# Streaming attention and a max-out MLP on one core: flags through a one-row matmul, batch 0's evacuations shared out anew, and another order for the weight preparation

## The chip, the cores and the metric

The kernel runs on one core of a Trainium2 chip. The time is the device time of one execution in microseconds (us), as the median of several runs. The profile is of a single further execution, and its times are counted from the first instruction. The engines are TensorE (PE, with its weight loads PEld), VectorE (DVE), ScalarE (ACT), GpSimd (POOL) and SyncE (SP, which here only issues transfers).

## The reference

There are 4 batches, 8 heads, 768 positions and 64 numbers per head. For every batch and head:

```
scores = q k^T / 8
mask   = causal                                          (retrieval heads)
       = causal and (key < 4 or query - key < 64)        (all other heads)
a      = softmax(scores where mask, else -1e9)
x      = a v
```

The heads of a position are joined to a row of 512 numbers, which makes 3072 rows. Then come the weights w1 and w2 (512 x 1024) and w_out (1024 x 512):

```
out = max(x w1, x w2) w_out
```

Which heads are retrieval heads is an input (`is_retrieval`, 8 numbers of 64 bits). All inputs and the output are 32-bit floats in HBM.

## The kernel before, in words

**Algebra.** max(h1, h2) is written as relu(x (w1 - w2)) + x w2. So the MLP needs only one up-projection, with `w12 = w1 - w2`, and the term x w2 w_out is folded into the down-projection by the product `w2o = w2 w_out`. Both are made on the chip from the loaded weights: `cast_w` makes bf16 copies `w2b` and `wob`, `diff_w` makes the four row blocks of `w12`, `prep_w2t` transposes `w2b` on TensorE (8 steps of 4 transposes, tile `pw`, then `w2t`), and `prep_w2o` multiplies (4 steps of 8 matmuls of 512 columns, tile `pw2`, shown as `pw` in the profile).

**Attention.** The work goes by pairs of heads: 16 pairs, numbered 0 to 15, four to a batch. q, k and v of a pair are loaded by SP (`qn`, `kn`, `vn`, four buffers each), cast to bf16 (`cast_qk`, `cast_v`), and q and k are turned so that the 64 numbers of a head lie on partitions. For pairs 0 to 7 `turn` does this with six transposes on TensorE and an evacuation from PSUM by `evac` (tile `qkt`; first q with dst 0, then k with dst 1); for pairs 8 to 15 `turn_qk` does it with a transposing DMA on SP's queue. Only the 21 of 36 blocks of 128 x 128 on or under the diagonal are computed, in six chunks (`CHUNKS`) of four blocks, one of them of a single block. Chunk t is chunk t mod 6 of pair t // 6. Its steps are `scores` (TensorE, PSUM tile `ps`, two buffers), `expo` (ScalarE, tile `at`, six buffers), `mask` (VectorE, for the first four chunks of a pair) and `weighted` (TensorE, PSUM tile `po`, with a column of ones for the sum of each row); after the second and the sixth chunk `normalise` (VectorE) writes `x`.

**Masks.** `masks(h)` makes one head's table `msk` as `tab_a * r[h] + tab_b`, with `tab` a constant table that is loaded once and `r` the head's flag, the same on all 128 partitions. For blocks far from the diagonal v itself is scaled: `vf = vb * rj` (GpSimd).

**MLP.** `turn` (batch 0 and the last pair) or `turn_x` (a transposing DMA on SP) makes `xt`, the rows x with their 512 numbers on partitions. A batch has two groups of 384 rows. `up` (8 steps to a group, 4 matmuls of 384 columns each, tile `ph`) is evacuated with a relu into `g`; `down` (3 blocks of 128 rows to a group, 12 matmuls of 512 columns each, in four parts of three, tile `pout`) adds x w2o and g wob, is evacuated into `ot` and stored by SP.

**Order.** Everything is issued in program order, by hand; each engine and SP's queue take their instructions strictly in that order. Chunks are pipelined two ahead. Batch 0 runs alone (t from 0 to 23). From batch 1 on a small planner (`fill`, `step`) puts parts of the MLP of the batch before between the chunks: `shorts` are single steps and `longs` are the down-projections; a down-projection is not begun while a short of the same number waits. `turns` are turns that wait for one of two PSUM banks. `evac` gives each evacuation to VectorE or ScalarE, whichever has been given less estimated time so far.

Between batch 0 and batch 1 the kernel before does, in this order: two `prep_w2t` steps within each of t = 20 to 23; the loads of pairs 4 to 7; the four differences; one product step; the turn of batch 0's last x; the other three product steps; the 8 ups of the first group; casts and turns of pair 4. The 8 ups of the second group and all downs are left to the planner.

Of the kernel before, what the change touches and what calls it, by code (L numbers as in the profile page):

```python
# [34 lines left out]
def kernel(  # L35
# [56 lines left out]
    ident = tab[:, 0:128]  # L92
    tab_a = tab[:, 130:642]
    tab_b = tab[:, 642:1154]
    ir = consts.tile([128, 2 * H], I32)
    flag = consts.tile([128, 2 * H], F32)
    r = consts.tile([128, H], F32)
    rj = consts.tile([128, H, 4], BF16)
    sink = consts.tile([128, 1], F32)
# [33 lines left out]
        given["s"] += us  # L133
        return nc.scalar

    def evac(out, in_, cols, relu=False):
        if given["v"] <= given["s"]:
            eng = vec(0.16 + cols / 960)
            if relu:
                eng.tensor_scalar_max(out=out, in0=in_, scalar1=0.0)  # L140
            else:
                eng.tensor_copy(out=out, in_=in_)  # L142
        else:
            sca(0.2 + cols / 1300).activation(  # L144
                out=out, in_=in_, func=ACT.Relu if relu else ACT.Copy
            )
# [39 lines left out]
    def turn(n, dst, bank):  # L186
        s = st[n]
        src = s["qk"][:, dst] if dst is not None else s["x"]
        pt = bank("pt").bitcast(BF16)
        for i in range(NB):  # L190
            nc.tensor.transpose(  # L191
                pt[:, i * 128:(i + 1) * 128],
                src[:, i].rearrange("p h d -> p (h d)"), ident,
            )
        if dst is None:
            b, p = pairs[n]
            if p == 0:
                xts[b] = xtp.tile([128, KC, S], BF16, tag="xt", name="xt")
            t = xts[b][:, p, :]
        else:  # L200
            if dst == 0:
                s["qkt"] = qktp.tile([128, 2, S], BF16, tag="qkt", name="qkt")
            t = s["qkt"][:, dst]
        pt = pt[:, 0:S]
        if dst is not None:
            pt = pt.rearrange("p (n t) -> p t n", n=NB)
            t = t.rearrange("p (t n) -> p t n", n=NB)
            evac(t, pt, S)
        else:
            evac(t, pt, 400)  # L210

    def cast_qk(n, e, eng):
        s = st[n]
# [162 lines left out]
    def bank_d(name):  # L376
        return psum_m.tile([128, 512], F32, tag="m1", name=name)
# [124 lines left out]
    def masks(h):  # L502
# [6 lines left out]


    ir_handle = bass.AP(
        tensor=_as_int32(is_retrieval, 2 * H), offset=0, ap=[[0, 128], [1, 2 * H]]
    )
    nc.scalar.dma_start(out=ir, in_=ir_handle)
    load_one(0, "qn", q, nc.sync)
    nc.scalar.dma_start(out=tab, in_=table_dram.ap())
    load_one(0, "kn", k, nc.sync)
    load_one(0, "vn", v, nc.sync)
    for n in range(1, HP):
        load_pair(n)  # L520
    load_w(moe_w2, w2f, 0, 2)
    load_w(moe_w2, w2f, 2, 4)
    load_w(moe_w_out, wof, 0, 4)
    load_w(moe_w_out, wof, 4, 8)
    for kc in range(KC):
        load_w(moe_w1, w1f, kc, kc + 1)

    nc.vector.tensor_single_scalar(out=flag, in_=ir, scalar=0.0, op=ALU.not_equal)
    halves = flag.rearrange("p (h two) -> p h two", two=2)
    nc.vector.tensor_tensor(out=r, in0=halves[:, :, 0], in1=halves[:, :, 1], op=ALU.max)  # L530
    nc.vector.tensor_copy(out=sink, in_=tab[:, 128:129])
    nc.vector.tensor_scalar(
        out=rj[:, :, 0], in0=r, scalar1=sink, scalar2=None, op0=ALU.max
    )
    nc.vector.tensor_copy(
        out=rj[:, :, 1:4], in_=r.unsqueeze(2).to_broadcast([128, H, 3])
    )
    masks(0)
    cast_qk(0, 0, nc.vector)
    turn(0, 0, bank_a)  # L540
    cast_qk(0, 1, nc.vector)
    turn(0, 1, bank_d)
    masks(1)
    masks(2)
    cast_v(0, nc.gpsimd)
    masks(3)
    cast_qk(1, 0, nc.vector)
    cast_qk(1, 1, nc.gpsimd)

    T = NCH * len(pairs)  # L550
    T0 = NCH * HP

    def side(t, last, first_batch):
# [8 lines left out]
                turns.append((0.34, lambda bank: turn(m, 1, bank), 0))  # L562
        if m + 1 < last:
            if m + 1 < LONG and c == 5:
                cast_qk(m + 1, 0, nc.vector)
                cast_qk(m + 1, 1, nc.gpsimd)
            if m + 1 >= LONG and c == 2:
                cast_qk(m + 1, 0, nc.gpsimd)
                cast_qk(m + 1, 1, nc.gpsimd)
# [21 lines left out]
    for t in range(T0):  # L591
# [13 lines left out]
        if t == 15:  # L605
            for kc in range(KC):
                cast_w(nc.gpsimd, w2b, w2f, kc, kc + 1)
            for f2 in range(4):
                cast_w(nc.gpsimd, wob, wof, 2 * f2, 2 * f2 + 2)
        if 20 <= t:  # L610
            for fc in range(2 * (t - 20), 2 * (t - 20) + 2):
                prep_w2t(fc, (bank_a, bank_d)[fc % 2])
    weighted(T0 - 1)
    for n in range(HP, HP + 4):
        load_pair(n)
    diff_w(nc.gpsimd, 0)
    diff_w(nc.gpsimd, 1)
    diff_w(nc.vector, 2)
    diff_w(nc.vector, 3)
    prep_w2o(0, bank_d)  # L620
    turn(HP - 1, None, bank_a)
    for kc in range(1, KC):
        prep_w2o(kc, six[kc + 1])
    given["v"] = given["s"] = 0.0
    for e, u in enumerate(ups(0, 0)):
        u[1](six[e % 6])
    n = HP
    cast_qk(n, 0, nc.vector)
    cast_qk(n, 1, nc.vector)
    turn(n, 0, bank_a)  # L630
    turn(n, 1, bank_d)
    cast_v(n, nc.vector)
    cast_qk(n + 1, 0, nc.vector)
    cast_qk(n + 1, 1, nc.gpsimd)

# [5 lines left out]
                + sum(u[0] for u in turns))  # L641

    longs += downs(0, 0) + downs(0, 1)
    shorts += ups(0, 1)
    fill(1.3)
    scores(T0)
    scores(T0 + 1)
    expo(T0)
    fill(0.65)
    expo(T0 + 1)  # L650
    mask(T0)
    mask(T0 + 1)
# [84 lines left out]
```

## Time and profile before

| | |
|---|---|
| median of 3 runs | 221.22 us (221.1 to 221.78) |
| profiled execution, its own time | 222.22 us |
| its span, first to last instruction | 220.4 us |
| mean granted TensorE clock | 0.969 |
| TensorE busy | 187.3 us (85%) |
| VectorE busy | 121.6 us (55%) |
| ScalarE busy | 114.2 us (52%) |
| GpSimd busy | 66.0 us (30%) |

An engine is busy while one of its own instructions runs; issuing transfers and waiting are not counted. The profile names an instruction by its line and its tiles, as out<-in. A row of a timeline holds the start, the duration, the engine (with q for the queue that only issues), the line, the operation, the tiles, the shapes, the count, and in brackets how long the engine had been idle and what released it. A row of the busy time by stretch holds the stretch and its length, then for PE, PEld, DVE, ACT and POOL the busy time and the number of instructions, and at the end the granted clock of TensorE, the busy share of the DMA engines and GB/s.

### The profile page before, as it was taken

Reading aid. Unit: us, or ns where it says so; the run is one execution under the profiler, and the core shown is the slowest. Engines: PE = TensorE matmul, PEld = TensorE weight load, DVE = VectorE, ACT = ScalarE, POOL = GpSimd, SP = SyncE. Lnnn points to the kernel's source line nnn. Section 1 sums busy time; section 2 is a strip of 40 time slices with the busy share of each in tenths; the row PEclk is TensorE's granted clock in tenths of the full one; section 3 lists DMA queues with packets and bytes.
Section 4 is the critical chain, followed back from the end, with each engine's and each line's share of the span. In section 5 each row is a group of like instructions: output and inputs, shape, how many; then the busy total and the mean of one; then the engine's idle time right before and its main releaser. Section 6 shows DMA issues by size and latency. Waiting matters only on the chain.

```text
span 220.4 us, 4437 instructions
## 1 busy us (share of the span) xinstructions
PE 187.3 (85%) x1822; PEld 105.9 (48%) x1822; DVE 121.6 (55%) x222; ACT 114.2 (52%) x150; POOL 66.0 (30%) x72
## 2 busy tenths in 40 slices
PE   0268968499958889994999999999999999899993
PEld 0234745274534546552545555555545555455441
DVE  0699857964347769657286565666373631342101
ACT  2087898423347786885534566593644651232120
POOL 1194549940046082516064143315110000000000
PEclk9999999859999999999599999999999999999999
DMA  3999999995000939999999999979531331200222
GB/s 102 313 293 319 396 398 384 288 292 136 0 0 3 220 77 210 141 215 190 223 220 207 224 203 232 261 145 206 146 83 50 83 85 48 95 0 3 95 95 95
DMA packets 81300, 37.36 MB, mean 169 GB/s; under 512 B 71936, under 2 KB 76032, under 8 KB 81280
## 3 DMA queue, kind: packets, MB, share of 16 engines
q1 hardware_dynamic: 80992, 36.77, 72.4%
q8 instruction: 14, 0.23, 0.5%
q10 hardware_dynamic: 288, 0.30, 0.4%
q14 instruction: 6, 0.05, 0.1%
HBM read 25.47 MB, written 6.29 MB: 144 GB/s over the span
## 4 chain that ended last, share of the span: by engine, by line
PE 64%; DVE 14%; DMA 7%; ACT 6%; issue 4%; SPq 2%; POOL 0%; ACTq 0%; POOLq 0%; DVEq 0%
PE pout L357 25%; PE ph L340 18%; PE po L304 8%; PE ps L254 7%; ACT at L267 5%; PE pw L487 3%; DVE at L285 3%; DMA tab<-mask_table 3%; DVE msk L503 3%; PE pt L191 2%; DMA qn<-in_q_dram 2%; DMA qkt<-qk 2%; DVE x L321 2%; DVE at L289 1%; DVE qk L219 1%
## 5 line engine op out<-in xcount | busy, mean ns | idle before, releaser
L267 ACT ACTIVATE at<-ps 128x1024 bf16<-128x1024 f32 x96 | 83.7, 919 | 36.4 <-PE ps L254 35.9
L340 PE MATMUL ph<-xt,w 128*128 128x384 bf16 x256 | 48.6, 329 | 2.4 <-ACT qkt L144 1.4
L357 PE MATMUL pout<-wob,g 128*128 128x512 bf16 x192 | 49.1, 383 | 0.0
L254 PE MATMUL ps<-qkt 64*128 64x256 bf16 (+1 forms) x416 | 32.1, 267 | 9.8 <-ACT at L267 4.0
L285 DVE TENSOR_TENSOR at<-at,msk 128x1024 bf16<-128x1024 bf16 (+2 forms) x48 | 31.7, 665 | 14.8 <-ACT at L267 14.8
L179 POOL TENSOR_TENSOR vf<-vb,rj 128x520 bf16<-128x520 bf16 x16 | 18.1, 1134 | 52.5 <-PE po L304 34.6
L140 DVE TENSOR_SCALAR g<-ph 128x384 bf16<-128x384 f32 x37 | 20.6, 556 | 23.5 <-PE ph L340 23.3
L340 PEld LDWEIGHTS <-w 128*128 128x128 bf16 x256 | 23.9, 98 | 19.7 <-issue 4.9
L304 PEld LDWEIGHTS <-at 128*128 128x128 bf16 x672 | 26.3, 102 | 12.3 <-issue 7.9
L254 PEld LDWEIGHTS <-qkt 64*128 64x128 bf16 x416 | 16.4, 97 | 27.5 <-issue 17.2
L357 PEld LDWEIGHTS <-g 128*128 128x128 bf16 x192 | 18.6, 99 | 19.2 <-issue 0.8
L357 PE MATMUL pout<-w2o,xt 128*128 128x512 bf16 x96 | 26.6, 379 | 0.1
L142 DVE COPY ot<-pout 128x512 f32<-128x512 f32 x16 | 11.1, 692 | 24.3 <-PE pout L357 23.7
L144 ACT ACTIVATE g<-ph 128x384 bf16<-128x384 f32 x27 | 13.3, 491 | 21.6 <-PE ph L340 20.6
L304 PE MATMUL po<-vb,at 128*128 128x65 bf16 x352 | 20.2, 200 | 1.6 <-DVE at L285 1.4
L304 PE MATMUL po<-vf,at 128*128 128x65 bf16 x320 | 19.4, 202 | 0.0
L191 PE MATMUL pt<-tab,qk 128*128 128x128 bf16 x96 | 9.7, 254 | 11.4 <-DVE qk L219 11.4
L321 DVE TENSOR_TENSOR x<-po,rez 128x384 bf16<-128x384 f32 x32 | 17.8, 558 | 2.1 <-DMA xt<-x 1.1
L177 POOL CAST vb<-vn 128x768 bf16<-128x768 f32 x15 | 14.4, 961 | 10.0 <-DMA vn<-in_v_dram 10.0
L144 ACT ACTIVATE ot<-pout 128x512 f32<-128x512 f32 x8 | 4.8, 597 | 21.1 <-PE pout L357 21.1
L219 POOL CAST qk<-qn 128x768 bf16<-128x768 f32 x8 | 6.6, 823 | 29.1 <-DMA qn<-in_q_dram 26.4
L144 ACT ACTIVATE qkt<-pt 128x768 bf16<-128x768 bf16 x12 | 9.5, 811 | 10.9 <-PE pt L191 10.8
(39 smaller groups left out, 120.6 us busy)
## 6 DMA issues: line engine op xcount, KB each, us to landing
qn<-in_q_dram SPq DMA_DIRECT2D x16, 384.0 KB, 5.4
kn<-in_k_dram SPq DMA_DIRECT2D x16, 384.0 KB, 5.7
vn<-in_v_dram SPq DMA_DIRECT2D x16, 384.0 KB, 6.4
out_dram<-ot SPq DMA_DIRECT2D x24, 256.0 KB, 2.1
w2f<-in_moe_w_dram SPq DMA_DIRECT2D x2, 1024.0 KB, 8.8
wof<-in_moe_w_out_dram SPq DMA_DIRECT2D x2, 1024.0 KB, 12.2
w1f<-in_moe_w_dram SPq DMA_DIRECT2D x4, 512.0 KB, 13.2
tab<-mask_table ACTq DMA_DIRECT2D x1, 288.5 KB, 6.7
```

The lines of the kernel that those rows point to most:

```text
L140: eng.tensor_scalar_max(out=out, in0=in_, scalar1=0.0)
L144: sca(0.2 + cols / 1300).activation(out=out, in_=in_, func=ACT.Relu if relu else ACT.Copy)
L177: eng.tensor_copy(out=vb[:, :, :, 0:D], in_=s["vn"])
L179: nc.gpsimd.tensor_tensor(out=vf, in0=vb[:, :, 0:4, :], in1=rj[:, 2 * p:2 * p + 2, :].unsqueeze(3).to_broadcast([128, 2, 4, D + 1]), op=AL ...
L191: nc.tensor.transpose(pt[:, i * 128:(i + 1) * 128], src[:, i].rearrange("p h d -> p (h d)"), ident,)
L254: nc.tensor.matmul(ps[:, hh, e * 128:(e + m) * 128], lhsT=s["qkt"][rows, 1, j * 128:(j + 1) * 128], rhs=s["qkt"][rows, 0, i * 128:(i + m) ...
L267: sca(0.13 + 2 * w / 1300).activation(out=at.rearrange("p h e c -> p h (e c)")[:, :, 0:w], in_=s["ps", c][:, :, 0:w], func=ACT.Exp, scale= ...
L285: eng.tensor_tensor(out=at, in0=at, in1=mk, op=ALU.mult)
L304: nc.tensor.matmul(s["po", half][:, hh, col, :], lhsT=at[:, hh, e, :], rhs=rhs, start=first, stop=(c == (LO_DONE, HI_DONE)[half]), skip_gr ...
L321: vec(0.55).tensor_tensor(out=s["x"][:, 3 * half:3 * half + 3].rearrange("p i h d -> p h i d"), in0=po[:, :, :, 0:D], in1=rez.unsqueeze(3) ...
L340: nc.tensor.matmul(ph, lhsT=w12[:, kc, fc * 128:(fc + 1) * 128], rhs=xts[b][:, kc, tg * GT:(tg + 1) * GT], start=(kc == 0), stop=(kc == KC ...
L357: nc.tensor.matmul(pout, lhsT=lhsT, rhs=rhs, start=(e == 0), stop=(e == len(steps) - 1),)
```

## The change

- *Flags.* The flags are loaded as one row instead of being loaded once per partition, behind the mask table on ScalarE's queue instead of ahead of it. VectorE reduces the one row to 8 flags, a matmul with a row of ones copies them to all partitions, and VectorE copies the result to `r`. The small tables `rj` are made after the first table `msk` and the first cast instead of ahead of them, and the tables of pairs' heads 2 and 3 come later.
- *Batch 0.* Its turns are no longer shared out by estimated time: q is evacuated by ScalarE, k and x by VectorE. The q casts of pairs 2 and 3 go from VectorE to GpSimd.
- *Loads.* On SP's queue w1 comes ahead of w_out, and pair 4's q, k and v come between them.
- *Weights.* The differences are made during batch 0 (two on GpSimd in t = 15, two on VectorE in t = 21 and 22), the casts of w_out after it.
- *Between the batches.* The ups of both groups come first (16 instead of 8), with the transposes of `w2b` and the turns of pair 4 strewn among the last eight. The four product steps become shorts for the planner, in the place of the second group's ups; the downs of the first group wait for them. The two fills around the first scores of batch 1 are gone.

```diff
--- before.py
+++ after.py
@@ -92,8 +92,10 @@
     ident = tab[:, 0:128]
     tab_a = tab[:, 130:642]
     tab_b = tab[:, 642:1154]
-    ir = consts.tile([128, 2 * H], I32)
-    flag = consts.tile([128, 2 * H], F32)
+    ir = consts.tile([1, 2 * H], I32)
+    flag = consts.tile([1, 2 * H], BF16)
+    flag_h = consts.tile([1, H], BF16)
+    ones = consts.tile([1, 128], BF16)
     r = consts.tile([128, H], F32)
     rj = consts.tile([128, H, 4], BF16)
     sink = consts.tile([128, 1], F32)
@@ -133,8 +135,10 @@
         given["s"] += us
         return nc.scalar
 
-    def evac(out, in_, cols, relu=False):
-        if given["v"] <= given["s"]:
+    def evac(out, in_, cols, relu=False, on_vector=None):
+        if on_vector is None:
+            on_vector = given["v"] <= given["s"]
+        if on_vector:
             eng = vec(0.16 + cols / 960)
             if relu:
                 eng.tensor_scalar_max(out=out, in0=in_, scalar1=0.0)
@@ -205,9 +209,9 @@
         if dst is not None:
             pt = pt.rearrange("p (n t) -> p t n", n=NB)
             t = t.rearrange("p (t n) -> p t n", n=NB)
-            evac(t, pt, S)
+            evac(t, pt, S, on_vector=dst == 1 if n < HP else None)
         else:
-            evac(t, pt, 400)
+            evac(t, pt, 400, on_vector=True if n < HP else None)
 
     def cast_qk(n, e, eng):
         s = st[n]
@@ -509,43 +513,49 @@
 
 
     ir_handle = bass.AP(
-        tensor=_as_int32(is_retrieval, 2 * H), offset=0, ap=[[0, 128], [1, 2 * H]]
+        tensor=_as_int32(is_retrieval, 2 * H), offset=0, ap=[[0, 1], [1, 2 * H]]
     )
+    nc.scalar.dma_start(out=tab, in_=table_dram.ap())
+    load_one(0, "qn", q, nc.sync)
     nc.scalar.dma_start(out=ir, in_=ir_handle)
-    load_one(0, "qn", q, nc.sync)
-    nc.scalar.dma_start(out=tab, in_=table_dram.ap())
     load_one(0, "kn", k, nc.sync)
     load_one(0, "vn", v, nc.sync)
     for n in range(1, HP):
         load_pair(n)
     load_w(moe_w2, w2f, 0, 2)
     load_w(moe_w2, w2f, 2, 4)
+    for kc in range(KC):
+        load_w(moe_w1, w1f, kc, kc + 1)
+    load_pair(HP)
     load_w(moe_w_out, wof, 0, 4)
     load_w(moe_w_out, wof, 4, 8)
-    for kc in range(KC):
-        load_w(moe_w1, w1f, kc, kc + 1)
-
+
+
+    nc.vector.memset(ones, 1.0)
     nc.vector.tensor_single_scalar(out=flag, in_=ir, scalar=0.0, op=ALU.not_equal)
     halves = flag.rearrange("p (h two) -> p h two", two=2)
-    nc.vector.tensor_tensor(out=r, in0=halves[:, :, 0], in1=halves[:, :, 1], op=ALU.max)
+    nc.vector.tensor_tensor(out=flag_h, in0=halves[:, :, 0], in1=halves[:, :, 1], op=ALU.max)
+    pr = bank_d("pr")[:, 0:H]
+    nc.tensor.matmul(pr, lhsT=ones, rhs=flag_h, start=True, stop=True)
+    nc.vector.tensor_copy(out=r, in_=pr)
     nc.vector.tensor_copy(out=sink, in_=tab[:, 128:129])
+    masks(0)
+    cast_qk(0, 0, nc.vector)
+    turn(0, 0, bank_a)
     nc.vector.tensor_scalar(
         out=rj[:, :, 0], in0=r, scalar1=sink, scalar2=None, op0=ALU.max
     )
     nc.vector.tensor_copy(
         out=rj[:, :, 1:4], in_=r.unsqueeze(2).to_broadcast([128, H, 3])
     )
-    masks(0)
-    cast_qk(0, 0, nc.vector)
-    turn(0, 0, bank_a)
     cast_qk(0, 1, nc.vector)
     turn(0, 1, bank_d)
     masks(1)
-    masks(2)
     cast_v(0, nc.gpsimd)
-    masks(3)
     cast_qk(1, 0, nc.vector)
     cast_qk(1, 1, nc.gpsimd)
+    masks(2)
+    masks(3)
 
     T = NCH * len(pairs)
     T0 = NCH * HP
@@ -562,7 +572,7 @@
                 turns.append((0.34, lambda bank: turn(m, 1, bank), 0))
         if m + 1 < last:
             if m + 1 < LONG and c == 5:
-                cast_qk(m + 1, 0, nc.vector)
+                cast_qk(m + 1, 0, nc.gpsimd if first_batch else nc.vector)
                 cast_qk(m + 1, 1, nc.gpsimd)
             if m + 1 >= LONG and c == 2:
                 cast_qk(m + 1, 0, nc.gpsimd)
@@ -605,31 +615,37 @@
         if t == 15:
             for kc in range(KC):
                 cast_w(nc.gpsimd, w2b, w2f, kc, kc + 1)
-            for f2 in range(4):
-                cast_w(nc.gpsimd, wob, wof, 2 * f2, 2 * f2 + 2)
-        if 20 <= t:
-            for fc in range(2 * (t - 20), 2 * (t - 20) + 2):
-                prep_w2t(fc, (bank_a, bank_d)[fc % 2])
+            diff_w(nc.gpsimd, 0)
+            diff_w(nc.gpsimd, 1)
+        if t in (21, 22):
+            diff_w(vec(1.2), t - 19)
     weighted(T0 - 1)
-    for n in range(HP, HP + 4):
+    for n in range(HP + 1, HP + 4):
         load_pair(n)
-    diff_w(nc.gpsimd, 0)
-    diff_w(nc.gpsimd, 1)
-    diff_w(nc.vector, 2)
-    diff_w(nc.vector, 3)
-    prep_w2o(0, bank_d)
     turn(HP - 1, None, bank_a)
-    for kc in range(1, KC):
-        prep_w2o(kc, six[kc + 1])
     given["v"] = given["s"] = 0.0
-    for e, u in enumerate(ups(0, 0)):
-        u[1](six[e % 6])
     n = HP
-    cast_qk(n, 0, nc.vector)
-    cast_qk(n, 1, nc.vector)
-    turn(n, 0, bank_a)
-    turn(n, 1, bank_d)
-    cast_v(n, nc.vector)
+    banks = [six[(e + 1) % 6] for e in range(26)]
+    for e, u in enumerate(ups(0, 0) + ups(0, 1)):
+        u[1](banks.pop(0))
+        if e == 3:
+            cast_qk(n, 0, nc.vector)
+            cast_qk(n, 1, nc.gpsimd)
+        if e == 11:
+            turn(n, 0, banks.pop(0))
+        if e == 13:
+            turn(n, 1, banks.pop(0))
+            cast_v(n, nc.gpsimd)
+        if e >= 8 and e not in (11, 13):
+            prep_w2t(e - 8 - (e > 11) - (e > 13), banks.pop(0))
+        if e == 5:
+            cast_w(nc.gpsimd, wob, wof, 0, 2)
+            cast_w(nc.gpsimd, wob, wof, 2, 4)
+        if e == 13:
+            cast_w(nc.gpsimd, wob, wof, 4, 6)
+            cast_w(vec(0.7), wob, wof, 6, 8)
+    prep_w2t(6, banks.pop(0))
+    prep_w2t(7, banks.pop(0))
     cast_qk(n + 1, 0, nc.vector)
     cast_qk(n + 1, 1, nc.gpsimd)
 
@@ -641,12 +657,10 @@
                 + sum(u[0] for u in turns))
 
     longs += downs(0, 0) + downs(0, 1)
-    shorts += ups(0, 1)
-    fill(1.3)
+    shorts += [(1.75, lambda bank, kc=kc: prep_w2o(kc, bank), 0) for kc in range(KC)]
     scores(T0)
     scores(T0 + 1)
     expo(T0)
-    fill(0.65)
     expo(T0 + 1)
     mask(T0)
     mask(T0 + 1)
```

## Prediction

> **What bounds the kernel now.** I read the page first, then the busy time by stage, the clock windows, and the timelines where TensorE is idle.
>
> ```profile
> PE 187.3 (85%) x1822; PEld 105.9 (48%) x1822; DVE 121.6 (55%) x222; ACT 114.2 (52%) x150; POOL 66.0 (30%) x72
> ...
> PEclk9999999859999999999599999999999999999999
> ```
>
> TensorE is busy 187.3 of 220.4 us and the change leaves its work as it is (one small matmul more). So a gain can only come out of the 33 us in which it is idle and out of the two dents in its granted clock. The stages, cut at the first scores, the last mask of batch 0, the first scores of batch 1, the first scores of pair 9, and the start of the tail:
>
> ```profile
> 0.00:12.06 12.06, 1.46 (x12) 1.20 (x14) 4.42 (x11) 2.79 (x3) 2.23 (x11) 1.00 0.78 214
> 12.06:44.17 32.11, 23.72 (x316) 15.59 (x317) 27.61 (x42) 24.96 (x30) 23.07 (x20) 0.98 1.10 348
> 44.17:66.26 22.09, 19.38 (x131) 11.54 (x132) 10.83 (x20) 7.06 (x12) 4.68 (x4) 0.88 0.41 106
> 66.26:105.19 38.93, 33.06 (x431) 19.37 (x431) 27.66 (x52) 29.06 (x35) 16.53 (x18) 0.99 0.88 154
> 105.19:190.28 85.09, 83.29 (x798) 45.01 (x799) 45.06 (x89) 44.09 (x58) 19.51 (x22) 0.97 0.81 157
> 190.28:220.40 30.12, 26.35 (x136) 13.16 (x135) 5.98 (x10) 6.21 (x12) 0.00 (x0) 1.00 0.17 61
> ```
>
> After the times come PE, PEld, DVE, ACT and POOL. The start has 10.6 us of idle TensorE, batch 0 8.4, the weight stage 2.7, the first part of batch 1 5.9; from 105.19 on TensorE is full, so whatever is won or lost before pair 9 goes straight to the end. In batch 0 VectorE (27.61 of 32.11) is fuller than ScalarE (24.96). The windows around the two clock dents (same columns, granted clock third from the end):
>
> ```profile
> 39.39:42.80 3.41, 1.86 (x34) 1.25 (x31) 3.38 (x5) 1.46 (x2) 3.41 (x3) 1.00 1.13 311
> 42.80:46.20 3.40, 1.65 (x16) 1.55 (x16) 2.88 (x5) 0.59 (x1) 3.40 (x2) 0.50 1.10 273
> 46.20:49.62 3.42, 3.34 (x32) 2.47 (x30) 2.00 (x5) 1.19 (x2) 0.17 (x1) 0.50 1.16 291
> 100.83:104.24 3.41, 0.88 (x24) 0.60 (x18) 2.33 (x5) 1.94 (x2) 2.86 (x3) 1.00 1.32 158
> 104.24:107.66 3.42, 2.47 (x23) 1.38 (x23) 0.97 (x2) 1.82 (x2) 0.00 (x0) 0.50 0.94 220
> ```
>
> Each dent follows a window in which TensorE was busy 1.86 or 0.88 us of 3.41, and ends after a nearly full one. What starves TensorE there, from the timelines:
>
> ```profile
> 41.68 4.70 POOL L500 TENSOR_TENSOR w<-w1f,w2f 128x1024 bf16<-128x1024 f32 x2
> 41.89 2.28 DVE L285 TENSOR_TENSOR at<-at,msk 128x256 bf16<-128x256 bf16 x1
> ```
>
> ```profile
> 89.34 0.36 SPq L365 DMA_DIRECT2D out_dram<-ot  x1
> ...
> 97.93 2.58 SPq L236 DMA_TRANSPOSE xt<-x  x1
> 100.69 2.50 SPq L226 DMA_TRANSPOSE qkt<-qk  x1
> ...
> 105.19 1.04 PE L254 MATMUL ps<-qkt 64*128 64x256 bf16 x10 [3.48 <-DMA qkt<-qk]
> ```
>
> A mask product that takes 0.28 us at 20.62 takes 2.28 while GpSimd subtracts weights beside it: VectorE stands until the GpSimd instruction ends. Pair 9's scores wait 3.48 us for a transpose that stands in SP's queue behind stores, loads and other transposes.
>
> **Start.** The table's DMA lands at 7.93 behind 128 flag descriptors. Issued first it should land about 1 us earlier. The flags, now one descriptor behind it, are not in the trace; bounds: 3.3 (issue at 1.2 plus the stores' 2.1) and 8.3 (the table's old landing plus 0.4). I take 6.2, since they move 64 bytes. Flag and maximum (0.17 each), the matmul's round trip (about 0.55: 0.14 from VectorE to TensorE at 9.5, 0.31 for a transpose at the slow clock, 0.1 back), two copies 0.3: first mask at 7.2-7.4, not 8.36. These wait in VectorE's queue with the q cast behind them, so the late bound would put the k cast at 11.0 and the first scores at 13.4. But kn lands only at 8.79, so the k cast starts at 8.85 (9.49 before); turn 0.82, VectorE's evacuation 0.94, while q's runs on ScalarE (before, both there, 1.51). First scores at 11.2, not 12.06: gain 0.85.
>
> **Batch 0.** ScalarE gives up three qkt evacuations and one xt: 3x0.81 + 0.80 = 3.2 us. VectorE takes them at 3x0.94 + 0.55 = 3.4, gives two q casts (2x0.55) to GpSimd, where they take 0.82 and have four idle us before them. So load goes to the fuller engine, and in VectorE's queue k of pair 1 now waits behind six mask tables and two mask products, most of them at 1.3 us beside GpSimd: pair 1's scores (19.39) come about 3.6 late, its first exponential at 23.5 (20.04). It is mostly won back: up to chunk 12 ScalarE has two evacuations less (1.6) and 1.4 of idle time, so that exponential (28.83) comes at 29.9; pair 3's turn no longer waits for the q cast at 30.53 nor for a bank (0.69), so chunk 18's mask (37.01) comes at 36.4. Then GpSimd's two differences (2.37 each), which held one mask before, stand at 37.0 to 41.8, as the wob casts moved behind them: masks 19 and 20 end at 39.5 and 41.9, then xt 0.55, normalise 0.76, mask 0.28: last mask at 43.4 (44.17). Bounds: 41.9 with neither mask held, 47.8 if none of the 3.6 comes back.
>
> **Weight stage.** VectorE's two differences (1.15 from start to start) hold the last normalise: 45.7, plus 0.8, and with nothing left to cover it TensorE waits; the turn of x at half clock takes 0.8: first up at 47.3. Then 16 ups x 0.65 = 10.4, 32 transposes of w2b x 0.06 = 1.9 (six take 0.36 in batch 1), two turns 0.7, and 1.2 for the half clock until 49.62 (one window more of it: 1.7 more). The waits for the q/k casts and qkt (1.12 + 1.13) go, as ups cover them. First scores at 61.5, not 66.26: 4.75 earlier. Evacuations (10 on VectorE, 16 on ScalarE, 0.4 to 0.95 each) and the wob casts fit beside 13 us of TensorE. Pair 4's load, ahead of wof on SP, waits only for buffers free since 10.4; wof lands some 4 us later (33.3 before), needed at about 50.
>
> Owed later: the product, 32x0.216 = 6.9, for seven ups (4.55) and three downs (0.65) already done: 3.0. And the two fills between the first scores are gone: chunk 26 waits a whole exponential (1.0) where 0.67 of idle time and 1.3 of work stood: 0.75 more idle. Net to pair 9: 4.75 - 3.0 - 0.75 = 1.0 gain.
>
> **SP's queue.** No down ends until the product is done, so pair 8's loads go out near 52 (71.76 before), and one store instead of three stands before its transpose. But two stores now stand right before xt and pair 9's transpose; the second is finished 6.3 us of TensorE work before pair 9's scores. Behind it: evacuation behind exponentials 1.5, store 0.4, xt 1.25, gaps 0.3, transpose 4.45 to landing: 7.9-8.0. Stall 1.7 instead of 3.48: gain 1.8; bounds 0 and 3.5.
>
> A 1.7 us stall inside one window leaves it busy 0.50, under the 0.55 that brought the first dent, so the dent stays; split over two windows it goes, worth 2.9 (5.87 us at half speed after 105.19). [...]
>
> **Sum.** 1.0 + 1.8 = 2.8: span 217.6, profiled execution 219.4 (222.22 before, 1.8 around the span). The median of the runs, 221.22, stands 1.0 below the profiled one: 218.4.
>
> **Rivals.** *The dent goes too* (stall under about 1.2 us, or split): for it, loads that go out 20 us earlier; against it, the store behind a late evacuation. 218.4 - 2.9 = 215.5.
> *VectorE keeps batch 0 back*: k's evacuation in its queue makes pair 1's scores 3.6 late and nothing wins it back. For it, VectorE full from 10 to 20 us; against it, ScalarE's idle time and 2.23 us of VectorE's own at 27.69. 218.4 + 3.6 = 222.0, slower; it decides once chunk 18's mask comes 2.8 us later than forecast, after 39.2.
> *The store holds pair 9 as long as before* (stall 3.5) and the half clock in the ups lasts one window more (1.7): 218.4 + 1.8 + 1.7 = 221.9, no change that can be told.
> That the change does less than it says: 8 of batch 0's 12 evacuations are VectorE's, 4 remain on ScalarE; it is in the counts.
>
> **Chances.** Forecast 0.40, dent gone 0.28, VectorE late 0.20, store as before 0.12. About 0.3% (0.66 us) is what can be told from no change. Faster 0.67 (forecast and dent gone, less 0.05 of their late ends, plus part of the store's case), same 0.10, slower 0.23 (VectorE late and the ends of the others). Range 214.9 (dent gone, 0.6 less) to 222.6 (VectorE late, plus part of the late flags).
>
> **What would show it.** Right: mask 0 near 7.3, pair 1's scores near 23, the last mask near 43.4, first ups at 47.3 at half clock, first scores of batch 1 near 61.5 with no gap before them, pair 9 after a stall of 1 to 2 us. Wrong: a last mask after 46; the flags landing after the table with VectorE idle; ups waiting for banks; a new stall at pairs 5 to 8; clock windows other than the two.

## The result

The kernel after takes 218.44 us (median; 218.17 to 221.5) beside 221.2 for the kernel before: ratio 0.9866, interval 0.9844 to 0.9887, so 1.3% faster. The forecast was 218.4.

The profiled execution of the kernel after is one of its longer ones (221.5 us, mean granted clock 0.942, where the executions behind the median had 0.952 to 0.961), so about two windows of half clock that it shows are not in the median. From its page, the busy time of the engines and the granted clock in 40 slices:

```profile
PE 187.9 (86%) x1801; PEld 106.3 (48%) x1823; DVE 124.4 (57%) x222; ACT 111.1 (51%) x149; POOL 69.7 (32%) x75
...
PEclk9999998555996999999699999999999999999998
```

TensorE's work is unchanged, as forecast; the first dent in the clock is much longer, the one near 104 us shorter, and there is a new one between them. The busy time by stage, cut at the same events as before (first scores, last mask of batch 0, first scores of batch 1, first scores of pair 9, start of the tail):

```profile
0.00:9.60 9.60, 1.67 (x13) 1.22 (x14) 3.60 (x12) 2.09 (x2) 2.38 (x11) 1.00 0.90 250
9.60:44.59 34.99, 25.04 (x308) 15.89 (x308) 32.70 (x45) 22.82 (x27) 25.32 (x22) 0.89 1.10 340
44.59:64.71 20.12, 17.10 (x132) 11.04 (x133) 12.04 (x17) 7.04 (x15) 8.76 (x8) 0.76 0.68 148
64.71:105.55 40.84, 36.48 (x429) 20.46 (x435) 26.37 (x52) 29.45 (x37) 13.07 (x14) 0.96 0.72 122
105.55:189.44 83.89, 81.31 (x788) 44.50 (x802) 43.76 (x90) 43.49 (x57) 20.18 (x22) 0.98 0.80 158
```

Set against the stages of before, in us: start 12.06 to 9.60, batch 0 32.11 to 34.99, weight stage 22.09 to 20.12, first part of batch 1 38.93 to 40.84, the rest 85.09 to 83.89. Three stages gain 5.6, two lose 4.8. VectorE is now busy 32.70 of batch 0's 34.99. In the timeline of the start:

```profile
4.96 0.16 DVE L535 TENSOR_SCALAR flag<-ir 1x16 bf16<-1x16 int32 x1 [3.97 <-DMA ir<-in_is_retrieval_dram]
...
5.76 0.75 DVE L507 SCALAR_TENSOR_TENSOR msk<-tab,r 128x512 bf16<-128x512 bf16 x1
...
7.12 0.55 DVE L223 CAST qk<-kn 128x768 bf16<-128x768 f32 x1
```

The first table starts at 5.76 (8.36 before), with the table landed at 4.09 (7.93 before). The cast of the first k starts at 7.12 (9.49), with kn landed at 6.05 and not at 8.79. The end of batch 0 and the weight stage, from the timelines of the three engines:

```profile
35.92 5.14 POOL L504 TENSOR_TENSOR w<-w1f,w2f 128x1024 bf16<-128x1024 f32 x2
36.02 2.83 DVE L289 TENSOR_TENSOR at<-at,msk 128x1024 bf16<-128x1024 bf16 x1
...
44.52 3.83 DVE L504 TENSOR_TENSOR w<-w1f,w2f 128x1024 bf16<-128x1024 f32 x2
...
48.48 0.56 DVE L325 TENSOR_TENSOR x<-po,rez 128x384 bf16<-128x384 f32 x1
...
49.10 0.50 PE L195 MATMUL pt<-tab,x 128*128 128x128 bf16 x3 [2.96 <-DVE x L325]
```

The mask of chunk 18 lasts 2.83 us beside the first of GpSimd's differences (0.69 at 29.39, with GpSimd idle). VectorE's own two differences then last 3.83, and TensorE waits 2.96 for the last x, which stands behind them. The windows around the later dents (third column from the end: granted clock):

```profile
64.43:67.84 3.41, 1.80 (x26) 1.11 (x24) 2.21 (x5) 3.41 (x6) 0.00 (x0) 1.00 0.00 0
67.84:71.25 3.41, 3.19 (x13) 1.38 (x11) 1.02 (x2) 0.80 (x2) 0.00 (x0) 0.50 0.02 5
101.98:105.39 3.41, 1.52 (x28) 0.92 (x26) 2.35 (x5) 2.35 (x4) 0.94 (x1) 1.00 1.10 234
```

And the timeline of SP's queue before pair 9, with TensorE's wait for it:

```profile
95.69 2.71 SPq L369 DMA_DIRECT2D out_dram<-ot  x2
98.49 1.25 SPq L240 DMA_TRANSPOSE xt<-x  x1
99.88 2.38 SPq L230 DMA_TRANSPOSE qkt<-qk  x1
...
105.55 0.71 PE L258 MATMUL ps<-qkt 64*128 64x256 bf16 x6 [2.04 <-DMA qkt<-qk]
```

Two stores stand before the transpose of x and that of pair 9, and TensorE waits 2.04 for it (3.48 before).

### The profile page after: what moved, and what is told of

Its sections match the earlier page's. It is cut to its first block, busy times and chain, and to the rows that moved or that the text cites. A ratio compares the mean times of both kernels' runs of the same rounds, so it can differ in the third digit from the quotient of the medians.

```text
span 219.7 us, 4420 instructions
## 1 busy us (share of the span) xinstructions
PE 187.9 (86%) x1801; PEld 106.3 (48%) x1823; DVE 124.4 (57%) x222; ACT 111.1 (51%) x149; POOL 69.7 (32%) x75
## 4 chain that ended last, share of the span: by engine, by line
PE 63%; DVE 18%; DMA 7%; ACT 5%; issue 3%; POOL 1%; SPq 0%; ACTq 0%; DVEq 0%
PE pout L361 23%; PE ph L344 18%; PE po L308 8%; PE ps L258 7%; DVE at L289 5%; ACT at L271 4%; PE pw L491 4%; PE pt L195 3%; DMA kn<-in_k_dram 3%; DMA qkt<-qk 3%; DVE msk L507 2%; DVE x L325 2%; DVE at L293 2%; DMA ir<-in_is_retrieval_dram 2%; DVE w L504 2%
## 5 line engine op out<-in xcount | busy, mean ns | idle before, releaser
L271 ACT ACTIVATE at<-ps 128x1024 bf16<-128x1024 f32 x96 | 84.0, 920 | 41.3 <-PE ps L258 39.2
L344 PE MATMUL ph<-xt,w 128*128 128x384 bf16 x256 | 50.5, 337 | 0.8 <-DVE xt L146 0.6
L361 PE MATMUL pout<-wob,g 128*128 128x512 bf16 x183 | 46.4, 380 | 0.9 <-issue 0.2
L289 DVE TENSOR_TENSOR at<-at,msk 128x1024 bf16<-128x1024 bf16 (+2 forms) x48 | 30.5, 639 | 13.7 <-ACT at L271 13.7
L308 PEld LDWEIGHTS <-at 128*128 128x128 bf16 x672 | 26.4, 103 | 19.1 <-DVE at L289 8.7
L144 DVE TENSOR_SCALAR g<-ph 128x384 bf16<-128x384 f32 x33 | 18.2, 555 | 28.5 <-PE ph L344 28.5
L148 ACT ACTIVATE g<-ph 128x384 bf16<-128x384 f32 x31 | 15.2, 490 | 30.4 <-PE ph L344 29.3
L361 PE MATMUL pout<-w2o,xt 128*128 128x512 bf16 x86 | 24.2, 381 | 0.9 <-DVE g L144 0.6
L223 POOL CAST qk<-kn 128x768 bf16<-128x768 f32 x15 | 13.9, 923 | 16.9 <-PE pt L195 10.7
L181 POOL CAST vb<-vn 128x768 bf16<-128x768 f32 x16 | 15.4, 962 | 7.3 <-DMA vn<-in_v_dram 7.3
L223 POOL CAST qk<-qn 128x768 bf16<-128x768 f32 x10 | 8.9, 894 | 22.8 <-DMA qn<-in_q_dram 20.8
L293 DVE TENSOR_TENSOR at<-at,msk 128x1024 bf16<-128x1024 bf16 x16 | 16.1, 1008 | 0.0
```

Of the source, the lines that this page charges most:

```text
L148: sca(0.2 + cols / 1300).activation(out=out, in_=in_, func=ACT.Relu if relu else ACT.Copy)
L223: eng.tensor_copy(out=s["qk"][:, e], in_=src.rearrange("p h n d -> p n h d"))
L271: sca(0.13 + 2 * w / 1300).activation(out=at.rearrange("p h e c -> p h (e c)")[:, :, 0:w], in_=s["ps", c][:, :, 0:w], func=ACT.Exp, scale= ...
L289: eng.tensor_tensor(out=at, in0=at, in1=mk, op=ALU.mult)
L293: eng.tensor_tensor(out=at, in0=at, in1=mk.to_broadcast([128, 2, reps, per * 128]), op=ALU.mult)
L308: nc.tensor.matmul(s["po", half][:, hh, col, :], lhsT=at[:, hh, e, :], rhs=rhs, start=first, stop=(c == (LO_DONE, HI_DONE)[half]), skip_gr ...
```

## The experiments

Times are medians, ratios are to the kernel before, run on the same chip. The theory is that the parts are worth very different amounts: the start gives about 2 us, batch 0's evacuations cost 0.5 to 2, and the weight part with SP's queue gives the rest. The rivals: the early start is swallowed, undoing the evacuations costs time, the weight part brings nothing.

### The start alone

The kernel before with only the flags through the one-row matmul and the table first (the flags' part of the change's diff, and no other):

```diff
-    ir = consts.tile([128, 2 * H], I32)
+    ir = consts.tile([1, 2 * H], I32)
...
-    nc.scalar.dma_start(out=ir, in_=ir_handle)
-    load_one(0, "qn", q, nc.sync)
     nc.scalar.dma_start(out=tab, in_=table_dram.ap())
+    load_one(0, "qn", q, nc.sync)
+    nc.scalar.dma_start(out=ir, in_=ir_handle)
...
+    nc.tensor.matmul(pr, lhsT=ones, rhs=flag_h, start=True, stop=True)
+    nc.vector.tensor_copy(out=r, in_=pr)
```

> The kernel before with the flags part of the change alone: table first, flags as one row, copied by the one-row matmul; everything else as before. Theory: the 128 flag descriptors cost all the first loads time, so kn lands near 6.1 instead of 8.8, the first scores start near 9.7 instead of 12.1, and in the old order of batch 0 most of the 2.4 us stays: 219.0 to 219.8. Rival: batch 0 is bound by later loads and by VectorE, so the early start is swallowed: 220.8 to 221.3.

Measured: 218.93, ratio 0.9900 (0.9873 to 0.9927). First table at 6.12, kn landed at 6.33, first scores at 9.82. The busy time of its batch 0:

```profile
9.82:41.89 32.07, 23.64 (x316) 15.50 (x317) 27.57 (x42) 24.95 (x30) 23.05 (x20) 1.00 1.11 349
```

Batch 0 is as long as before (32.11), so the 2.24 us won at the start reach its end whole. This part alone is about three quarters of the change's gain.

The second kernel of this pair changes only the order: the flags still go out once per partition, behind the table and the first q.

```diff
-    nc.scalar.dma_start(out=ir, in_=ir_handle)
-    load_one(0, "qn", q, nc.sync)
     nc.scalar.dma_start(out=tab, in_=table_dram.ap())
+    load_one(0, "qn", q, nc.sync)
+    nc.scalar.dma_start(out=ir, in_=ir_handle)
```

> The kernel before with only the two transfers on ScalarE's queue exchanged: the table first, the flags behind it, still loaded once per partition. Theory that the descriptors cost, wherever they stand: kn lands at 8 or later as before, the flags land after the table at 7 to 8.5, VectorE starts its masks no earlier than before: 221.0 to 222.5. Rival, that the order is what counts: kn near 6.1 and the time near that of the flags part alone, 219 to 220.

Measured: 220.07, ratio 0.9957 (0.9932 to 0.9982). The table lands at 4.33, qn at 5.1, but the flags only at 6.7 and kn at 7.85. So neither forecast holds alone: the order gives somewhat under half of this gain, and the one row instead of 128 the rest: with it, kn lands at 6.33. The flags' small transfers delayed not only the table behind them (7.93 before, 4.33 here) but the loads of k, which another engine issues (8.79 before, 7.85 here).

### Batch 0's evacuations

The kernel after with the evacuations and q casts of batch 0 as before:

```diff
-            evac(t, pt, S, on_vector=dst == 1 if n < HP else None)
+            evac(t, pt, S)
-            evac(t, pt, 400, on_vector=True if n < HP else None)
+            evac(t, pt, 400)
-                cast_qk(m + 1, 0, nc.gpsimd if first_batch else nc.vector)
+                cast_qk(m + 1, 0, nc.vector)
```

> The changed kernel with batch 0's evacuations shared out by estimated time again and the q casts of pairs 2 and 3 back on VectorE; all else as changed. Theory of the prediction: the change put load on the fuller engine, so undoing it ends batch 0 earlier by 0.5 to 2 us: 216.5 to 218.0. Rival: VectorE's share frees ScalarE and TensorE, and undoing it costs 0.5 to 2: 219.0 to 220.5.

Measured: 217.30, ratio 0.9830 (0.9787 to 0.9874). The intervals of this and of the kernel after overlap, so the times alone do not settle the sign; the traces help. Busy time of its batch 0, and of the two windows around the first scores of batch 1:

```profile
9.06:42.99 33.93, 24.45 (x308) 15.93 (x308) 29.44 (x43) 24.95 (x30) 24.13 (x20) 0.91 1.10 340
...
60.95:64.36 3.41, 2.33 (x31) 1.62 (x29) 2.44 (x5) 3.41 (x7) 0.84 (x2) 1.00 0.00 0
64.36:67.77 3.41, 2.83 (x28) 1.50 (x25) 2.11 (x4) 1.83 (x3) 0.00 (x0) 1.00 0.02 5
```

Pair 1's first scores come at 17.11 instead of 19.79, and batch 0 is 1.06 shorter, with VectorE busy 29.44 instead of 32.70. Other kernels below confirm the sign: with GpSimd's differences whole, batch 0 takes 34.99 to 35.66 in five kernels with the new sharing and 33.60 to 33.93 in three with the old one. So this part of the change costs 1 to 2 us. There is no dent after the first scores of batch 1: the same stalls there fall into two windows, busy 2.33 and 2.83 of 3.41, where they fell into one of 1.80. That is not the evacuations' doing, as the kernel with the stores moved (below) has the new ones and no dent there either.

### The weight part alone

The kernel before with the new order of loads, the weight preparation and the order between the batches, and the start and evacuations as before:

```diff
+    for kc in range(KC):
+        load_w(moe_w1, w1f, kc, kc + 1)
+    load_pair(HP)
     load_w(moe_w_out, wof, 0, 4)
...
+            diff_w(nc.gpsimd, 0)
+            diff_w(nc.gpsimd, 1)
+        if t in (21, 22):
+            diff_w(vec(1.2), t - 19)
...
```

> The kernel before with only the order of loads and weight preparation of the change (both up-projections first, differences in batch 0, the product as filler); start, evacuations and casts as before. Theory of the prediction: the weight stage and SP's queue bring most of the gain, 1.0 + 1.8 less the start: 218.5 to 219.8, pair 9 stalls under 2.3 us. Rival: they bring nothing, as batch 0 loses by the GpSimd work and the half clock what the fill wins, and the gain is the start's: 220.8 to 222.

Measured: 219.53, ratio 0.9951 (0.9914 to 0.9987). The twelve times run from 218.62 to 221.98, and the profiled execution (221.82, clock 0.929) is near their upper end. In it the last mask comes at 45.22 (44.17 before), TensorE waits 2.96 for the last x, and the first scores of batch 1 come at 65.8 (66.26). So in this execution the rebuilt weight stage wins little by itself: the differences in batch 0 end it 1.05 later. The start alone times this part alone is 0.9900 x 0.9951 = 0.985, within the interval of the kernel without the new evacuations (0.983): the times agree with parts that add up.

### Covering the wait before the ups, and two other costs

Three kernels take one suspected cost each out of the kernel after. First, six transposes of w2 ahead of the turn of the last x:

```diff
+    for fc in range(6):
+        prep_w2t(fc, (bank_d, bank_a)[fc % 2])
     turn(HP - 1, None, bank_a)
...
-        if e >= 8 and e not in (11, 13):
-            prep_w2t(e - 8 - (e > 11) - (e > 13), banks.pop(0))
```

> The changed kernel with six of the eight transpose steps of w2b put ahead of the turn of batch 0's last x, where TensorE waits 2.96 us for VectorE, instead of among the last ups. Theory: that wait is uncovered and, lying in windows that are under 0.6 busy, it also keeps the clock at half into the ups, in some executions for a window more; the fill takes 1.5 us of work out of the ups' stage and ends the half clock a window (3.4 us) earlier: 215.5 to 217.5, and the executions lie closer together than those of the changed kernel. Rival: the half clock stays, as its windows are fixed by the wait for the masks before, and the evacuations of the transposes stand ahead of the last normalise: 218.0 to 219.5.

Measured: 219.23, ratio 0.9916 (0.989 to 0.9943): nothing won. The first up comes later (50.69 against 49.40), the first scores of batch 1 earlier (63.75 against 64.71), the dent after them remains (67.27 to 70.68), and so does the stall at pair 9 (2.02).

Second, three casts of w_out on ScalarE instead of GpSimd, which runs them beside VectorE's differences:

```diff
-            cast_w(nc.gpsimd, wob, wof, 0, 2)
-            cast_w(nc.gpsimd, wob, wof, 2, 4)
+            cast_w(sca(0.9), wob, wof, 0, 2)
+            cast_w(sca(0.9), wob, wof, 2, 4)
...
-            cast_w(nc.gpsimd, wob, wof, 4, 6)
+            cast_w(sca(0.9), wob, wof, 4, 6)
```

> The changed kernel with three of the four w_out casts on ScalarE, which idles 8.6 us there, instead of GpSimd. Theory: GpSimd's casts beside VectorE's two differences stretch these from 1.22 to 1.84 and 2.07 and hold the last mask by 0.67; without them the last normalise starts 1.5 to 2 us earlier: 216.5 to 217.5. Rival: pair 4's casts on GpSimd move up into the same place and hold VectorE as long: 218 to 219.

Measured: 221.92, ratio 1.0039 (1.0007 to 1.007). The theory falls in the trace (a timeline of VectorE):

```profile
45.10 3.60 DVE L504 TENSOR_TENSOR w<-w1f,w2f 128x1024 bf16<-128x1024 f32 x2
```

VectorE's differences last 3.60 instead of 3.83, and TensorE still waits 2.73 for the last x, because GpSimd's casts and products for the next pairs move up to 42.61 and stand beside them, as the rival said. The first scores of batch 1 come at about the same time (65.00). Where the time is lost is not shown: the profiled execution (224.79, above the median) has pair 7 at 92.17 instead of 89.98 and the tail at 192.81 instead of 189.44, and casts booked on ScalarE also change what `evac` gives to which engine afterwards.

Third, the stores of batch 0's rows issued by ScalarE:

```diff
-        nc.sync.dma_start(out=out[row:row + 128, :], in_=ot)
+        (nc.scalar if b == 0 else nc.sync).dma_start(out=out[row:row + 128, :], in_=ot)
```

> The changed kernel with the stores of batch 0's rows issued on ScalarE's queue instead of SP's, so that no store stands ahead of pair 9's transpose. Theory: the stall of 2.04 us at pair 9 is SP's order; it shrinks to under 0.7 and the half clock behind it goes: 215.5 to 217.5. Rival: the loads' backlog in the rings holds the transposes as long, the stall stays at 1.5 or more, and ScalarE now waits for VectorE's evacuations: 218 to 220.

Measured: 219.72, ratio 0.9925 (0.9887 to 0.9964); the profiled execution took 218.78, at clock 0.961. TensorE's wait at pair 9 is as good as gone:

```profile
103.11 0.40 PE L258 MATMUL ps<-qkt 64*128 64x256 bf16 x4 [0.24 <-ACT at L271]
```

and no window there has half clock. Yet the median is not better than that of the kernel after. The wait is SP's queue, as the forecast said, but most of it only changes its place: between the first scores of pair 8 and those of pair 9 TensorE idles 1.38 us instead of 2.10, now in waits of 0.51, 0.59 and 0.24 for exponentials, so 0.7 of the 2.04 is won there, and the times do not show it.

All of these with the evacuations undone (transposes first, casts on ScalarE, stores on ScalarE):

> The changed kernel with batch 0's evacuations as before, the six transpose steps ahead of the last turn, the w_out casts on ScalarE and batch 0's stores on ScalarE's queue. If each theory holds and half of the gains overlap: 212.5 to 215. If the evacuations alone count: 217.0 to 217.6.

Measured: 217.49, ratio 0.9854 (0.9815 to 0.9892), no better than the evacuations alone (217.30). The first scores of batch 1 are early (60.51), and a dent (63.97 to 67.38) takes part of it back.

### The fill between the first exponentials

The kernel after with one fill put back:

```diff
     expo(T0)
+    fill(0.65)
     expo(T0 + 1)
```

> The kernel after with one fill put back: a step of the product of the weights between the first two exponentials of batch 1. Theory A (the taken fills cost what the forecast said, and a little more): the three waits of 0.5 us each for the first exponentials are covered, the first 3.41-us window of batch 1 is full enough to keep the full clock, and the stretch from the first scores of pair 4 to those of pair 5 takes 8.3 us where it took 10.0: median 216.4 to 217.7, against 218.4. Rival B (in that stretch ScalarE's exponentials set the pace, so that TensorE's work there only changes its place): the stretch keeps its 10 us or gives it back by pair 8, median 218.1 to 218.9.

Measured: 220.62, ratio 0.9972 (0.9951 to 0.9993), about 2 us slower than without it. From pair 4's first scores to pair 5's it takes 8.19 us, against 10.02 in the profiled execution of the kernel after and 8.33 where that has no dent (evacuations undone). Then, from the timeline of TensorE in pair 5:

```profile
74.76 0.40 PE L258 MATMUL ps<-qkt 64*128 64x128 bf16 x6 [1.27 <-ACT at L271]
...
80.96 1.89 PE L491 MATMUL pw<-wob,w2t 128*128 128x512 bf16 x8 [0.86 <-DVE qkt L146]
```

Pair 5 takes 9.68 us to pair 6, not 7.46: the product step that now runs early is missing between pair 5's first scores, which wait 1.27 for an exponential. The idle time moves, and a new one (0.86, for an evacuation) is added. The theory that the fill's absence is a loss falls.

### GpSimd's differences in pieces

The kernel with the evacuations undone, and GpSimd's two differences of 1024 columns cut into four of 256 each:

```diff
-            diff_w(nc.gpsimd, 0)
-            diff_w(nc.gpsimd, 1)
+            for kc in range(2):
+                for h in range(4):
+                    cols = slice(256 * h, 256 * h + 256)
+                    nc.gpsimd.tensor_tensor(
+                        out=w12[:, kc, cols], in0=w1f[:, kc, cols], in1=w2f[:, kc, cols],
+                        op=ALU.subtract)
```

> The kernel after with batch 0's evacuations and q casts as before (the earlier run of that alone gave 217.3), and GpSimd's two differences cut into four instructions of 256 columns each. Theory A (VectorE's masks stand until the GpSimd instruction next to them ends, so it is the length of one instruction that counts): no mask product takes more than 1.0 us where one took 2.8, the mask of chunk 18 ends near 36 instead of 37.25, the last mask near 41.9 instead of 42.99, median 216.2 to 217.0. Rival B (what counts is the sum of GpSimd's time, and eight instructions cost more overhead than two): masks of 0.7 to 1.0 each, but more of them, last mask at 42.8 to 43.5, median 217.2 to 217.8.

Measured: 213.11, ratio 0.9632 (0.9591 to 0.9673). This is the largest single step of the study: 4.2 us less than with whole differences. Timelines of VectorE and GpSimd, whole (the kernel with the evacuations undone):

```profile
34.36 5.09 POOL L504 TENSOR_TENSOR w<-w1f,w2f 128x1024 bf16<-128x1024 f32 x2
34.73 2.52 DVE L289 TENSOR_TENSOR at<-at,msk 128x1024 bf16<-128x1024 bf16 x1 [1.24 <-ACT at L271]
...
37.87 1.87 DVE L289 TENSOR_TENSOR at<-at,msk 128x512 bf16<-128x512 bf16 x1
```

and in pieces:

```profile
34.47 7.63 POOL L621 TENSOR_TENSOR w<-w1f,w2f 128x256 bf16<-128x256 f32 x8
34.84 0.90 DVE L289 TENSOR_TENSOR at<-at,msk 128x1024 bf16<-128x1024 bf16 x1 [1.23 <-ACT at L271]
...
36.36 0.94 DVE L289 TENSOR_TENSOR at<-at,msk 128x512 bf16<-128x512 bf16 x1
```

GpSimd needs 2.5 us more for the same subtraction, but the masks take 0.90 and 0.94 instead of 2.52 and 1.87. The mask of chunk 18 ends at 35.74 instead of 37.25, the last mask at 39.85 instead of 42.99, which is more than either theory expected: half clock lasts two windows (40.30 to 47.13) instead of four (37.09 to 50.74), and the first scores of batch 1 come at 58.66 instead of 62.26. There is no wait at pair 9.

The three costs that lay apart, all taken out with whole differences (evacuations undone, fill back, stores on ScalarE):

> The kernel after with batch 0's evacuations and q casts as before, the one fill put back, and batch 0's stores issued by ScalarE instead of SP. Theory A (the three costs lie in different stretches and add up): evacuations 1.0, fill and the half clock after the first scores 1.0 to 1.7, pair 9's wait and the half clock after it 1.0 to 2.5: first scores of batch 1 near 62.3, pair 5 near 70.6, pair 9 near 99 without a wait for its transpose, median 214.3 to 216.4. Rival B (what the stores no longer hold is given back by ScalarE's own waits, as in the run with the stores alone, and the fill only moves work): 216.8 to 217.6, as with the evacuations alone.

Measured: 218.45, ratio 0.9864 (0.9838 to 0.9889), not faster than the evacuations alone (0.9830; the intervals overlap). Pair 9 comes at 103.91 without a wait, yet later than 101.05 with one: 1.00 of this is there at the first scores of batch 1, and pair 5 takes 9.68 again instead of 7.46 with the fill. The costs did not add up; the fill took back what the stores gave.

### A version that beats both

In pieces, three of the four row blocks on GpSimd, ahead of the casts of w2, and one on VectorE:

```diff
-            for kc in range(KC):
-                cast_w(nc.gpsimd, w2b, w2f, kc, kc + 1)
-            for kc in range(2):
+            for kc in range(3):
                 for h in range(4):
...
+            for kc in range(KC):
+                cast_w(nc.gpsimd, w2b, w2f, kc, kc + 1)
-        if t in (21, 22):
-            diff_w(vec(1.2), t - 19)
+        if t == 21:
+            diff_w(vec(1.2), 3)
```

> The kernel with the cut differences (213.1), with three of the four row blocks on GpSimd, twelve pieces, ahead of the casts of w2 instead of behind them, and only the last block on VectorE, right after the last mask. Theory A (VectorE's two differences are what the last x still waits for, 2.81 us of idle TensorE): the pieces run from 29.8 to about 41.2, VectorE's one block ends near 41.5, x at 42.2, first up at 42.6 to 43.0 instead of 44.23, and the time 211.0 to 212.3. Rival B (the pieces that now stand beside more of batch 0's masks slow these by as much, or the casts of w2, now in the ups' time, hold the ups' transposes): last mask after 40.8 or a gap before the first scores of batch 1, and 212.8 to 214.5.

Measured: 211.21, ratio 0.9561 (0.9517 to 0.9605). Timelines of VectorE and TensorE:

```profile
39.40 2.05 DVE L504 TENSOR_TENSOR w<-w1f,w2f 128x1024 bf16<-128x1024 f32 x1
...
42.21 0.50 PE L195 MATMUL pt<-tab,x 128*128 128x128 bf16 x3 [1.24 <-DVE x L325]
```

The wait before the ups is 1.24 instead of 2.81 with two blocks on VectorE, and the first up comes at 42.50. A wait of 1.47 for pair 9's transpose is back, without half clock behind it. The interval meets that of the two-block version, so the step between the two is shown by the trace more than by the times; against the kernel before, 4.4% are won.

## Why the prediction was right, and where its steps were not

The number was right in part by luck: terms that were off by 1 to 3 us cancelled. Stage by stage, forecast and profiled execution of after, in us: start 11.2 and 9.60; batch 0 32.2 (43.4 - 11.2) and 34.99; weight stage 18.1 and 20.12; first part of batch 1 40.9 and 40.84; the rest 85.09 and 83.89; tail 30.12 and 30.29. The differences are -1.6, +2.8, +2.0, -0.1, -1.2 and +0.2, together 2.1 on the span of 217.6: 219.7, where the executions behind the median have spans of 216.4 to 216.9.

The mean clocks suggest where these make up for it. A clock of 0.942 over 219.7 us is worth 7.5 windows of half clock (0.058 x 219.7 x 2 / 3.41), 0.961 over 216.4 us only 4.9. The kernel with the stores moved, at 0.961 too, shows five, all of them between 36.22 and 53.29, and its first scores of batch 1 come at 64.51, as late as here. So the executions behind the median most likely lose the same 3.2 us in the first three stages and have neither of the two later dents. The forecast kept one dent, at 2.9, and made its absence a rival with a chance of 0.28. No trace of such an execution of this kernel exists, so this is an inference. The forecast's own sign of being wrong, clock windows other than the two, did appear in the profile.

- **Start.** Forecast 0.85, measured 2.46. The step that failed is "kn lands only at 8.79", taken over from before. It landed at 6.05; with the flags still sent once per partition, but behind the table, it landed at 7.85, so their 128 transfers held the other loads too. The flags landed at 4.9, within the bounds of 3.3 and 8.3 but earlier than the 6.2 taken, and from there to the first table it took 0.80 where 1.0 to 1.2 were costed.
- **Batch 0.** From the first scores to pair 1's it took 7.33 before and 10.19 after, so 2.9 were lost (3.6 forecast). The step that failed is "mostly won back": the mask of chunk 18 was to start 25.2 after the first scores (36.4 - 11.2; 24.95 before) and started 26.4 after them, so only about half came back. It was also to be done before GpSimd's differences, at 37.0; these start at 35.92 and hold it for 2.83 us (0.69 alone), then the next mask for 1.87 (0.74 alone), and GpSimd's casts of w_out hold the last mask for 0.95 (0.28 alone). So the last mask ended at 44.59 instead of 43.4, although batch 0 began 1.6 earlier. The rival, VectorE keeping batch 0 back by 3.6, was to show in chunk 18's mask coming after 39.2. It started at 36.02, and undoing the new sharing wins 1 to 2 us, so that rival falls in its size, though its mechanism is part of the loss. More of the loss hangs on the length of GpSimd's instructions, as the pieces showed.
- **Weight stage.** VectorE's differences were priced at 1.15 each, from a row where GpSimd was idle; beside GpSimd's casts and products they took 1.84 and 2.07. The wait of TensorE for x was named, and is 2.96. One window more of half clock was priced at 1.7 but not taken into the sum; it lasted to 54.19 instead of 49.62. From the last mask to the first up it took 4.81 (3.9 forecast), from there to the first scores of batch 1 15.31 (14.2): these are the 2.0 that are missing.
- **Owed later.** 3.75 was forecast for the product and the missing fills, more than twice what was measured. By stage: 40.84 less the stall of 2.04 and the new dent's 1.7, against 38.93 less 3.48, makes 1.65; with the evacuations undone, where there is no dent, 38.79 - 1.67 - 35.45 = 1.67. In the latter TensorE's busy time rose by 1.91 (33.06 to 34.97), not by 3.0, and the missing fills cost nothing (they cost time when put back). The dent at 67.84 was not foreseen; half of its 3.41 us, the 1.7 above, is an estimate of its cost, and makes up the difference.
- **SP's queue.** The stall was right: 1.7 forecast, 2.04 here, and 1.47 to 2.26 in six other kernels that keep SP's order and the new weight part; a seventh, with two blocks in pieces, has none. The dent after it stays in this profile, as forecast, but for one window instead of two, worth most of the 1.2 of the rest. The rival of the stall that lasts as long as before falls. That of the dent gone is open for the executions behind the median, as said above: no dent follows stalls of 1.77 (the fill put back) and 1.47 (three blocks), one follows 1.67 (evacuations undone).

## What to carry to other kernels

GpSimd's subtractions of 1024 columns beside VectorE's critical masks were worth cutting before anything was moved: beside pieces of 256 a mask took 0.90 us and not 2.52, and the 4.2 us won are more than the whole change made (2.8). The flags, 8 KB spread over 128 partitions, were not a small load when they went out first: kn landed at 8.79, at 7.85 with them behind the table, and at 6.33 with one row there; look at when the loads behind such a load land, on every queue. A stall's price depended on which clock windows it fell into: the stalls at the first scores of batch 1 were followed by 3.41 us of half clock where one window held them (busy 1.80), and by none where two did (2.33 and 2.83). So gains and losses of 1 to 2 us appear and vanish with a shift in time, and fills put back for a stall should be tested for what they take from the next one (here new waits of 1.27 and 0.86).

## What the runs showed of the hardware

- **VectorE beside GpSimd.** A mask of 0.68 us took 2.52 beside a GpSimd subtraction of 2.34, and ended 0.55 after it; the next subtraction, issued meanwhile, took 2.79. In pieces (0.72 the shortest) the same mask took 0.90. What helped was to make GpSimd's instruction short: the last mask ended at 39.85 instead of 42.99.
- **The clock's windows.** In the fourteen kernels' traces, each window of 3.41 us at full clock ahead of the tail in which TensorE was busy 1.86 us or less (25 windows, from 0.58 up) was followed by half clock, and none with more than 2.34 was. Between the two the rows go both ways. The first of these, from the kernel with three blocks on GpSimd, kept the full clock; after the second, from the weight part alone, it was halved:

```profile
94.25:97.66 3.41, 1.89 (x35) 1.09 (x32) 1.27 (x5) 2.73 (x4) 0.00 (x0) 1.00 0.91 173
35.17:38.58 3.41, 2.34 (x34) 1.45 (x33) 2.17 (x2) 3.41 (x4) 3.41 (x3) 1.00 1.03 337
```

So the busy time that a profile shows is not the whole rule. The way back is no clearer: a window of half clock with 2.60 busy brought the full clock (the start alone, 101.78), one with 3.15 did not (the weight part alone, 21.52). Ahead of the first change of clock on record (26.88 in after) the rows read 1.00, yet four matmuls of scores of the same shape take 0.61 us at 19.79, as they do at 40.10 in half clock, and 0.39 at 27.57, so the start was as slow there as half clock.

- **The flags.** Eight flags loaded once per partition, ahead of everything, went with a landing of k at 8.79 and 8.81 us (two kernels); once per partition behind the table, at 7.85; as one row behind the table, at 6.05 to 6.94 (eleven kernels).
